# Weight pieces requested from ScalarE's queue, and a new written-out order, in a fused linear-attention and gated-MLP kernel

## The chip, the cores and the metric

The kernel runs on one core of one Trainium2 chip. The metric is the time of one execution on the device, in microseconds (us). The time before is the median of three runs.

## The reference

Two blocks run one after the other, all inputs and outputs in float32.

```python
# block 1: gated linear attention; q, k, v, alpha are (B=4, H=8, S=768, D=48)
for t in range(S):
    state = alpha[:, :, t, :, None] * state + einsum('bhd,bhe->bhde', k[:, :, t], v[:, :, t])
    y[:, :, t] = einsum('bhd,bhde->bhe', q[:, :, t], state)
x = y.transpose(0, 2, 1, 3).reshape(B, S, H * D)          # (4, 768, 384)
# block 2: gated MLP with a spatial product
h = maximum(x @ w_in, 0)                                   # w_in (384, 1024)
u, v = h[..., :512], h[..., 512:]
v_n = (v - mean(v)) / sqrt(var(v) + 1e-6)                  # over the last axis
v_s = einsum('ts,bsd->btd', w_spatial, v_n) + b_spatial    # w_spatial (768, 768)
out = (u * v_s) @ w_out                                    # w_out (512, 384)
```

## The kernel before, in words

**Tiling.** The recurrence is cut into 24 chunks of 128 tokens, six for each of the four batches. The first eight chunks are worked as four pairs (function `pair`), whose loads bring two chunks at once; the other 16 are worked singly (function `first`). A chunk's path is: logarithm of alpha (`lnp` of a pair, `ln` of a single chunk, ScalarE), cumulated sums on TensorE (`cump` or `cum`), exponentials on ScalarE (`einvp`, `eexpp`), products with k and q (`ktp`, `qtp`), transposes of both (`tr.k`, `tr.q`) and their copies out of PSUM (`ev.k`, `ev.q`), scores (`sc`), a mask product on VectorE (`m`, L594 and L765), the output from the scores and v (`ya`), and the share of the state (`y`). The state goes from chunk to chunk by `updq` or `upd` (TensorE), `z` (VectorE, L337 and L339), `S` (a product on GpSimd, L344) and `sb` (its copy to bfloat16). `vbp` casts v. `xs`, `xt` and `xe` turn a chunk's output into the transposed input of block 2.

**Block 2.** Per batch: six groups `v` (three matmuls of 512 columns, L828), whose results get their statistics (`bn`) and are normalised (`rs`, `vn`); eight groups `u` (three matmuls of 384 columns); eight groups `s`, the spatial product (six matmuls of 384 columns, in two parts); a product `g` with u; six groups `o`, the output (four matmuls), and the stores. All these matmuls have line L828.

**Weights.** They come in six pieces of 768 KB: the two halves of `w_in` (`w_in.1`, read by `v`, then `w_in.0`, read by `u`), three thirds of `w_spatial` (`w_sp.0` to `w_sp.2`), and `w_out`. Each is requested by one DMA in `fetch` (L1081), lands in one of two buffers `raw_w`, and is cast to bfloat16 part by part (`cast.w_in.1.0` and so on). There are two buffers, so the third piece is requested when the casts of the first are done, and so on. Each third of `w_spatial` is then transposed on TensorE (`wt.0` to `wt.5`, L840) and copied out (`we`).

**The order.** Nothing is reordered at run time: each engine runs its instructions in the order in which the kernel emits them. That order is written out in the table `PLAN`, made offline; a function `replay` emits operation after operation. A word such as `A4` means operation 4 on ScalarE (P TensorE, D VectorE, A ScalarE, G GpSimd, S the sync engine SP with its queue of requests; Q words emit nothing). The table chooses the engine too where an operation may run on more than one. A suffix gives "junk" columns: `P53:512:512:192` puts three matmuls of those widths on a constant tile, in float32, in front of operation 53, into the PSUM bank that this operation is about to use (L187). They compute nothing that is used. The eight banks are handed out in turn, so an operation waits until the bank's user eight turns earlier is done.

Operations named in the prediction, with their numbers: `cump.0.1` 53, `bb.0` and `bb.1` (the bias row spread over the partitions) 247 and 249, `tr.q.0.0` 51, `S.0` 66, `cz.2` (constants of the single chunks) 3, `sb.0` 67, `sc.1.0` 131, `v.0.0` 85, `u.0.3.0` 155, `v.0.5` 215, `wt.2` 235, `w_in.1` to `w_out` requests 4, 9, 14, 18, 22, 26.

Of the kernel before, what the change touches and what calls it, by code (L numbers as in the profile page):

```python
# [54 lines left out]
LETTERS = {"P": "PE", "D": "DVE", "A": "ACT", "G": "POOL", "S": "SP", "Q": "DMA"}  # L55

PLAN = """
S34 Q35 S36 Q37 G32 G0 Q33 S38 Q39 S94 Q95 S40 Q41 A42 P53:512:512:192 A54 D1 D2 D56 P43 S96 Q97 S98 Q99 S100 Q101
S163 Q164 S4 Q5 S165 Q166 S167 Q168 P59:464 G58 G48 A44 A45 A55 D46 D57 D47 P249:304 P49 P61 A50 P51 D52 D60 A62 A102
A250 P71:304 P74 P113 P103 D72 D73 D76 D75 P63 P77:172 D65 A114 D116 P119:148 A104 A64 A115 A105 A78 G66 G67 G106 D107  # L60
D117 D68 P79 P81 P111 P121 P247 P109 G3 G69 A108 A82 A80 D120 D122 D112 D110 P83 A84 A171 D248 S169 Q170 S9 Q10 S307
Q308 P131 P134 D133 D136 D132 D135 G70 G118 P172:228 P182 P123:240 A183 A8 A173 A124 P137 P138 A139 A174 G7 G6 D125
P85 G126 D128 D185 G127 G129 G175 P88 P142 P140 A86 A184 D176 D186 A143 A89 P188 P190 P180 P144 P178 A141 A191 A145
A181 P146 G11 G12 S309 Q310 S311 Q312 D130 D87 D179 D90 D189 P157 A187 A177 A158 A147 A13 P197 P200 P192 D199 D201
D198 D194 D202 P151:196 P155 A315 A193 A91 P326 P316 A327 P203 P153 P204 G195 G196 G329 A317 A328 A318 P149 A205 A154
D159 D156 D152 D330 G319 P208 P334 A209 P206 D320 P332 P324 P210 P322 D92 D335 D325 D333 D148 A207 P212 A211 A150 P347
P215 P221 A213 A160 A222 A216 S14 Q15 P223 P227 S18 Q19 D93 D323 D161 D348 D349 D214 G16 G17 A224 A228 P225 P229 A226
A21 P232 A234 D231 D230 D233 G20 P235:300 P238 S313 Q314 G331 G321 P344 P336 S367 Q368 S369 Q370 S22 Q23 S371 Q372
A237 A236 D217 D162 D346 A240 D338 A239 A218 D219 D220 A375 A337 P251 P263 P259 P376 A377 A378 G339 P264 D345 D341
D265 P260 D261 P255 P252 A380 A25 A24 D381 D253 P256 D257 G340 G342 G379 S409 Q410 S373 Q374 S446 Q447 S411 Q412 S413  # L70
Q414 S415 Q416 S26 Q27 S480 Q481 S448 Q449 S482 Q483 S450 Q451 S484 Q485 P383 A385 A417 S452 Q453 S577 Q578 S486 Q487
S581 Q582 S579 Q580 S583 Q584 P244 P241 P350 A246 D384 D245 D242 D243 P390 P354 P418 D392 D391 A351 A355 G262 G343
A420 A382 G254 G266 P279 P352 P271 P356 P393 P272 A353 A357 A419 G421 A422 A394 P280 P361 P386 P275 P395 A362 A424
A396 A31 D273 D423 D281 D387 P425 D397 D427 D426 D363 G282 G388 P276 P358 D277 P398 G258 G389 G278 G30 A399 A454 A359
A28 A488 P405 P432 P267 P455 P401 A402 A457 A456 D29 P291 P489 P268 A490 A459 D406 D433 D400 D434 D360 P283 P428 D269
D460 A492 D429 D493 G458 G491 P435 A284 A292 A436 G274 G461 G270 G430 G431 S648 Q649 S617 Q618 S650 Q651 S611 Q612
S652 Q653 S613 Q614 S690 Q691 S615 Q616 S694 Q695 S654 Q655 S692 Q693 P287 P462 P437 P495 P403 D463 D464 D497 D496
A288 A439 A438 P440 A585 A441 A364 D404 P469 P498 P295 P465 P586 P303 D471 D470 D466 D500 D499 A296 A587 A588 A590
A304 P299 G494 G467 G468 G589 G592 D591 D442 P472 A473 P501 P407 P474 A502 A300 P503 P593 P596 A443 A505 A408 D475
D476 P477 A478 D504 D366 D594 D595 D445 D444 D597 D365 P506 P600 P515 D601 D516 A507 A479 A508 D509 D602 A656 A510  # L80
A619 P517 P525 P513 P519 P529 P657 P533 P620 D511 D512 P526 P530 A514 A659 A658 A621 A661 A622 A698 A624 D518 D520
D527 D531 D662 P545 P534 P699 A701 A700 A703 D625 G598 G599 G660 G626 G623 G528 D535 P546 D547 P630 P627 P664 P537
P603 D631 D665 D704 G548 A629 A628 G632 G663 A604 P538 P634 P605 S728 Q729 S762 Q763 S696 Q697 S730 Q731 S732 Q733
S764 Q765 S766 Q767 D539 A607 A666 A606 D635 D636 P541 P667 P542 G702 G532 P706 P671 D668 D543 D673 D672 G669 G536
G670 G544 G633 P608 P637 P521 A707 A736 A708 A638 P737 P713 P639 P522 P549 D714 D715 D641 D523 A770 A609 A705 A738
A739 G740 A640 A741 D742 P771 P550 P642 A772 P709 P744 A774 A643 A746 D710 D551 D775 D745 D644 G524 S858 Q859 S734
Q735 S929 Q930 S860 Q861 G773 G711 G552 G712 G743 G540 P716 P674 A717 A675 P561 P718 P676 P777 P553 A562 A678 A677
D719 D779 D720 D610 P679 P751 A778 A554 A866 A680 A645 A681 P780 D752 P747 D748 D753 D781 D782 P682 P867 P721 P754
A868 A869 A871 A722 A755 S768 Q769 S862 Q863 A723 A776 D683 D872 P573 P688 P684 G749 G750 G870 P756 P874 D646 D757
D875 D685 D758 A689 A574 D724 A876 P686 P783 P569 P881 A784 P785 A570 A787 A687 A725 D882 D786 D883 P759 P557 A760  # L90
P788 P565 P796 P798 P800 S1042 Q1043 S971 Q972 S892 Q893 S864 Q865 S898 Q899 S896 Q897 A979 A558 A789 A566 A937 A900
S894 Q895 S935 Q936 G873 S975 Q976 S931 Q932 S933 Q934 S973 Q974 S977 Q978 S1008 Q1009 S567 Q568 S1046 Q1047 S559 Q560
S1012 Q1013 S1010 Q1011 S1044 Q1045 S1014 Q1015 D727 D647 D761 D726 P794 P806 D790 A791 D799 D797 D795 D792 D793 D801
P901 P980 P802 P938 P877 P807 A902 A903 A907 A905 A981 A939 A940 A982 A944 A984 P810 P803 A942 G904 D878 G941 G879
D808 D906 D804 G805 G880 G809 G983 D985 D943 P822 P884 P811 D812 A885 P823 P908 P886 P945 D824 P814 P911 P815 D912
D909 D816 G813 G817 G913 G825 A910 A887 A888 A947 A946 P889 A1016 A890 P952 P915 P987 D953 D916 D954 P830 P1017 P831
P818 A988 A1019 A1050 A1018 D917 P948 P819 P1051 D949 A1021 A986 A989 D1022 D832 G950 P834 A1052 G951 G1020 P990 P842
P918 A835 A1054 D820 D991 D1055 A843 A919 P838 P1024 P994 P920 D1025 D921 D995 D996 A839 A1023 G914 G833 G1053 G992
S1048 Q1049 S575 Q576 S836 Q837 S844 Q845 S293 Q294 S289 Q290 S571 Q572 S305 Q306 S301 Q302 S555 Q556 A922 A1026 S297
Q298 S285 Q286 S840 Q841 P826 P955 P827 D828 A956 P1057 P957 P1031 D958 P1027 D1028 D1033 D1032 P997 P923 A1058 A1059  # L100
A959 P969 P1060 A1056 A998 P999 D1062 D1001 D1061 D970 G821 G829 G993 G1029 A1000 A924 P960 P846 P1034 A961 A847 G1030
P1063 A1035 A1064 P1002 P963 P1036 P1065 D925 D891 A1003 D962 D1066 P850 P967 A1067 A1037 D1004 A926 D928 P1068 A964
A1038 P1039 D927 D968 A851 A1005 A1069 A1040 D1006 D1041 D1007 D1070 P965 P854 P1076 P1080 P1078 P1074 D966 A1079 A855
A1071 A1081 D1075 D1072 D1073 D1077 P1094 P1082 P1106 P1086 P1083 P1098 P1095 P1090 P1102 P1087 P1107 P1091 P1103
P1110 P1099 P1111 D1096 D1084 G1085 D1088 D1097 D1108 D1092 D1093 G1089 P1113 D1104 G1109 G1105 D1112 D1100 D1101
P1117 P1121 S852 Q853 S563 Q564 S856 Q857 S848 Q849 A1114 S1115 Q1116 A1118 P1133 S1119 Q1120 A1122 P1125 A1134 S1123
Q1124 P1129 S1135 Q1136 A1126 P1137 S1127 Q1128 A1130 A1138 S1131 Q1132 S1139 Q1140
"""


# [13 lines left out]
def kernel(  # L124
# [12 lines left out]
    nc = tc.nc  # L137
# [19 lines left out]
    LD, LP, WT, ST = 1.03, 1.46, 2.35, 0.8  # L157
# [913 lines left out]
    fetched, casts = [], []  # L1071

    def fetch(key, prio, to, src):

        n, cols = src.shape[1], src.shape[2]
        hold = {}

        def load(_):
            flat = raws.tile([128, n * cols], FP32, name="raw_w")
            hold["w"] = flat.rearrange("p (n f) -> p n f", n=n)  # L1080
            nc.sync.dma_start(out=hold["w"], in_=src)  # L1081

        dma(key, WT, load, list(fetched[-NRAW] if len(fetched) >= NRAW else []), prio, issue=0.68)
        for j in range(n):
            tt = 2 * key[-1] + j if to is None else None

            def cast(eng, j=j, tt=tt):
                if to is None:
                    wsp_nat[tt] = raws.tile([128, S], BF16, name="w_row", bufs=NROW)
                copy(eng, wsp_nat[tt] if to is None else to[:, j, :], hold["w"][:, j, :])  # L1090

            op(("cast",) + key + (j,), {"POOL": 0.02 + 0.0012 * cols, "ACT": 0.11 + 0.00073 * cols, "DVE": 0.07 + 0.00104 * cols},
               None, cast, got(key), prio=prio + 12)
            if to is None:
                casts.append((made[("cast",) + key + (j,)], tt))
        made[key] = [made[("cast",) + key + (j,)] for j in range(n)]
        fetched.append(made[key])
# [59 lines left out]
```

## Time and profile before

| | |
|---|---|
| three runs | 143.14, 143.57, 144.17 us; median 143.57 |
| the profiled execution | 143.08 us, of which 141.3 us are the span from the first to the last instruction |
| granted TensorE clock | 1.000 of full |
| TensorE matmul busy | 133.2 us (94% of the span), of it 10.2 us on junk columns |
| VectorE, ScalarE, GpSimd busy | 118.3, 108.6, 83.4 us |
| bytes moved by DMA | 28.64 MB, mean 203 GB/s |

How to read it: busy times are sums of the stretches in which an engine had at least one instruction under way; the junk columns count as busy. Line numbers are those of the kernel file. Durations in the rows reach from an instruction's start to the end of its writes, so that two instructions of one engine can overlap a little.

### The profile page before, as it was taken

The numbers are of one execution on the slowest core, as the hardware profiler recorded it, in microseconds if no ns is written. First come the engines' busy times: TensorE is split into PE (matmuls) and PEld (weight loads), VectorE is DVE, ScalarE is ACT, GpSimd is POOL, SyncE is SP. The second block draws the span as 40 slices with busy tenths as digits, with TensorE's granted clock in tenths as the row PEclk, the third lists the DMA queues.
The fourth block names the chain that finished last, engine by engine and source line by source line (L and its number), as shares of the span: only waits on it lengthen the run. The fifth ranks groups of instructions, "written<-read, shape, count | busy, mean of one in ns | idle before, by whom it ended". The sixth has DMA issues, their size and how long they took to land.

```text
span 141.3 us, 4968 instructions
## 1 busy us (share of the span) xinstructions
PE 133.2 (94%) x1912; PEld 84.2 (60%) x1923; DVE 118.3 (84%) x291; ACT 108.6 (77%) x282; POOL 83.4 (59%) x146
## 2 busy tenths in 40 slices
PE   7989798999999999999999999999999989999990
PEld 3457575575667656565675665656666656566560
DVE  7479878999989599999998898989979779894940
ACT  3677569988989969889887999997889969940061
POOL 6722986293449596982299899500799993000720
PEclk9999999999999999999999999999999999999999
DMA  4999999999898989989799999979978690112044
GB/s 102 323 323 332 331 272 311 225 320 238 241 232 156 283 161 208 205 161 212 154 205 179 193 217 177 222 143 195 250 151 203 225 375 24 70 56 102 0 164 170
DMA packets 89000, 28.64 MB, mean 203 GB/s; under 512 B 83728, under 2 KB 87440, under 8 KB 88976
## 3 DMA queue, kind: packets, MB, share of 16 engines
q1 hardware_dynamic: 88944, 28.32, 81.6%
q8 instruction: 15, 0.25, 0.7%
q14 instruction: 9, 0.07, 0.2%
q0 software_dynamic: 32, 0.00, 0.0%
HBM read 23.60 MB, written 4.72 MB: 200 GB/s over the span
## 4 chain that ended last, share of the span: by engine, by line
PE 71%; DVE 9%; POOL 7%; issue 5%; ACT 4%; ACTq 0%; POOLq 0%; DVEq 0%
PE bank L828 47%; PE bank L187 4%; DVE ptm L594 3%; PE bank L719 2%; PE bank L754 2%; POOL sbd L199 2%; POOL gT L989 2%; PE bank L511 2%; PE bank L782 2%; DVE ptm L765 2%; PE bank L740 1%; PE bank L583 1%; POOL kt L690 1%; PE bank L666 1%; DVE kqT L199 1%
## 5 line engine op out<-in xcount | busy, mean ns | idle before, releaser
L828 PE MATMUL bank<-w_spT,vn 128*128 128x384 bf16 x192 | 36.8, 326 | 0.0
L989 POOL TENSOR_TENSOR gT<-vsb,uT 128x384 bf16<-128x384 f32 x28 | 25.7, 923 | 14.9 <-DVE vsb L976 14.4
L690 POOL TENSOR_TENSOR kt<-kc,binv 128x384 bf16<-128x384 f32 x16 | 14.6, 914 | 13.4 <-ACT bc L685 8.6
L765 DVE TENSOR_TENSOR ptm<-bank,mask 128x512 bf16<-128x512 f32 x32 | 20.7, 682 | 1.9 <-PE bank L398 1.2
L828 PEld LDWEIGHTS <-vn 128*128 128x128 bf16 x192 | 16.6, 97 | 9.5 <-issue 0.2
L976 DVE TENSOR_TENSOR vsb<-bank,bsp_bc 128x384 f32<-128x384 f32 x31 | 16.5, 551 | 4.2 <-PE bank L828 2.5
L828 PE MATMUL bank<-xT,w_in 128*128 128x384 bf16 x96 | 18.7, 326 | 0.0
L828 PE MATMUL bank<-w_out_sb,gT 128*128 128x384 bf16 (+1 forms) x100 | 18.7, 319 | 0.0
L828 PE MATMUL bank<-w_in,xT 128*128 128x512 bf16 x61 | 17.2, 379 | 0.8 <-issue 0.2
L344 POOL TENSOR_TENSOR state<-state,bc 128x192 f32<-128x192 f32 x20 | 10.4, 520 | 11.4 <-DVE state L337 5.4
L197 ACT COPY kqT<-bank 128x512 bf16<-128x512 bf16 x21 | 12.1, 599 | 3.9 <-PE bank L719 1.1
L199 POOL CAST sbd<-state 64x192 bf16<-64x192 f32 x38 | 13.3, 350 | 2.0
L893 DVE BATCH_NORM_STATS2 stats<-v_sb 128x6 f32<-128x512 bf16 x20 | 13.7, 683 | 0.3 <-ACT v_sb L203 0.3
L203 ACT ACTIVATE v_sb<-bank 128x512 bf16<-128x512 f32 x20 | 11.8, 605 | 1.4 <-PE bank L828 1.3
L197 ACT CAST x_sb<-bank 128x384 bf16<-128x384 f32 x24 | 11.4, 490 | 1.5 <-PE bank L623 1.3
L828 PEld LDWEIGHTS <-w_in 128*128 128x128 bf16 x96 | 8.8, 97 | 5.9
L828 PEld LDWEIGHTS <-gT 128*128 128x128 bf16 x100 | 8.9, 97 | 5.6 <-DVE gT L989 0.4
L199 DVE COPY kqT<-bank 128x512 bf16<-128x512 bf16 x27 | 10.5, 416 | 1.9 <-PE bank L511 1.0
L187 PE MATMUL bank<-junk 128*128 128x512 f32 (+9 forms) x24 | 10.2, 529 | 1.1 <-DVE junk L240 1.1
L594 DVE TENSOR_TENSOR ptm<-bank,mask 128x512 bf16<-128x512 f32 x16 | 10.2, 683 | 0.5 <-PE bank L583 0.4
L197 ACT COPY xT<-bank 128x192 bf16<-128x192 bf16 (+1 forms) x26 | 9.4, 379 | 1.6 <-PE bank L398 1.1
L197 ACT COPY o_sb<-bank 128x384 f32<-128x384 f32 x9 | 4.4, 484 | 8.0 <-PE bank L828 8.0
(126 smaller groups left out, 284.0 us busy)
## 6 DMA issues: line engine op xcount, KB each, us to landing
ac<-in_alpha_dram SPq DMA_DIRECT2D x16, 192.0 KB, 4.1
kc<-in_k_dram SPq DMA_DIRECT2D x16, 192.0 KB, 4.8
qc<-in_q_dram SPq DMA_DIRECT2D x16, 192.0 KB, 4.1
vc<-in_v_dram SPq DMA_DIRECT2D x16, 192.0 KB, 3.8
raw_w<-in_moe_w_spatial_dram SPq DMA_DIRECT2D x3, 768.0 KB, 6.8
out_dram<-raw_w SPq DMA_DIRECT2D x11, 192.0 KB, 2.5
out_dram<-o_sb SPq DMA_DIRECT2D x9, 192.0 KB, 1.8
ac<-in_alpha_dram SPq DMA_DIRECT2D x4, 384.0 KB, 5.0
```

Source lines behind the costliest of these rows:

```text
L187: nc.tensor.matmul(out=flat[:, 0:cols].rearrange("p (a b) -> p a b", a=4), lhsT=junk, rhs=junk[:, None, 0:n].to_broadcast([128, 4, n]), st ...
L197: nc.scalar.copy(out=out, in_=in_)
L199: ENG[eng].tensor_copy(out=out, in_=in_)
L203: nc.scalar.activation(out=out, in_=in_, func=AF.Relu)
L344: ENG[eng].tensor_tensor(out=st["state"], in0=st["state"], in1=st["bc"][:, :, None].to_broadcast([128, HP, D]), op=ALU.mult)
L594: nc.vector.tensor_tensor(out=st[f"ptm{par}"][:, s], in0=st[f"pt{s}{par}"], in1=mask2[:, par], op=ALU.mult)
L690: ENG[eng].tensor_mul(out=k_blocks(kt3)[:, :, :, 0:D], in0=quad(st["kc"]), in1=st["binv"])
L765: nc.vector.tensor_tensor(out=st["ptm"][:, s], in0=st[f"pt{s}"], in1=mask4, op=ALU.mult)
L828: return lambda ps: nc.tensor.matmul(out=out(ps), lhsT=lhsT(), rhs=rhs(), start=start, stop=stop)
L893: nc.vector.bn_stats(out=stats, in_=d["v_sb"][:, tt, :])
L976: nc.vector.tensor_tensor(out=hold["vs"], in0=ps[:, 0:TH], in1=bsp_bc[:, th, :], op=ALU.add)
L989: ENG[eng].tensor_tensor(out=bt[b]["gT"][:, dsl, cols], in0=hold["vs"], in1=bt[b]["uT"][:, dsl, cols], op=ALU.mult)
```

## The change

Two edits. First, the six requests for weight pieces are issued by ScalarE, on ScalarE's own queue of requests, and no longer by SP; the table's maker is told 0.43 us for such a request instead of 0.68. Second, `PLAN` is a new table over the same 1141 operations. By its description the maker of the table now counts the time in which VectorE is held by GpSimd, and places junk columns by the gaps of the new order. Of the operations that may run on several engines, 12 copies `ev` move from VectorE to ScalarE and 8 the other way, 8 `u` to ScalarE and 2 back, 8 small `xe` to ScalarE and 7 back, 4 copies `sb` and 3 products `g` from GpSimd to VectorE and one of each back, and 4 weight casts from ScalarE to GpSimd. The junk suffixes after the first are 464, 304, 304, 172, 148, 228, 240, 196 and 300 columns before, the last at `wt.2`; after, they are 512:512:512 at `tr.q.0.0`, then 320, 292, 224 and 204, the last at `sc.1.0`.

```diff
@@ PLAN, its first lines
-S34 Q35 S36 Q37 G32 G0 Q33 S38 Q39 S94 Q95 S40 Q41 A42 P53:512:512:192 A54 D1 D2 D56 P43 S96 Q97 S98 Q99 S100 Q101
-S163 Q164 S4 Q5 S165 Q166 S167 Q168 P59:464 G58 G48 A44 A45 A55 D46 D57 D47 P249:304 P49 P61 A50 P51 D52 D60 A62 A102
-A250 P71:304 P74 P113 P103 D72 D73 D76 D75 P63 P77:172 D65 A114 D116 P119:148 A104 A64 A115 A105 A78 G66 G67 G106 D107
-D117 D68 P79 P81 P111 P121 P247 P109 G3 G69 A108 A82 A80 D120 D122 D112 D110 P83 A84 A171 D248 S169 Q170 S9 Q10 S307
...
+G32 G0 S34 Q35 D2 Q33 S38 Q39 D1 S36 Q37 S94 Q95 S40 Q41 A42 P247:512:512:192 P249 A250 P53 S96 Q97 P43 A54 A55 A248
+S98 Q99 A44 A45 D46 S163 Q164 A102 D47 D57 P51:512:512:512 D56 S100 Q101 P61 A48 G58 A52 P63:320 S167 Q168 P59 D65 P49
+D62 A60 S165 Q166 A50 P74:292 A64 P103 A4 Q5 D76 G66 P71 S169 Q170 A171 G3 D72 A104 D68 S307 Q308 D73 A105 G106 P113
+P172 D75 A114 P182 G67 D107 A183 G69 D116 A173 P111:224 P109 A115 P77 A184 G108 D117 P81 G7 D112 A78 A174 G6 S311 Q312
+D186 P79 P119 A80 D176 G118 P190 A82 D120 G8 P121 S309 Q310 D110 P180 A122 G175 D181 A191 D185 P131:204 G70 P83 P85
...
@@ fetch, load
-            nc.sync.dma_start(out=hold["w"], in_=src)
-
-        dma(key, WT, load, list(fetched[-NRAW] if len(fetched) >= NRAW else []), prio, issue=0.68)
+            nc.scalar.dma_start(out=hold["w"], in_=src)
+
+        dma(key, WT, load, list(fetched[-NRAW] if len(fetched) >= NRAW else []), prio, "ACT", 0.43)
```

## The prediction

> **What bounds the kernel now.** I read the page's first two parts, then the chain that ended last, then stretches of the span, then the waits.
>
> ```profile
> span 141.3 us, 4968 instructions
> PE 133.2 (94%) x1912; PEld 84.2 (60%) x1923; DVE 118.3 (84%) x291; ACT 108.6 (77%) x282; POOL 83.4 (59%) x146
> PEclk9999999999999999999999999999999999999999
> ```
>
> TensorE is busy 94% of the span, at full granted clock. Its end decides: in the chain, in order of time, the last long piece is TensorE alone, and after it come one copy and the last store.
>
> ```profile
> 120.12 17.56 PE bank L828 x105
> 137.72 0.31 issue
> ```
>
> Stretches of five and twenty us, with their sum, then TensorE, weight loads, VectorE, ScalarE and GpSimd; the first group is everything, the second only the junk matmuls of L187:
>
> ```profile
> 25.00:30.00 5.00, 4.66 (x103) 3.17 (x103) 4.93 (x12) 4.42 (x12) 1.92 (x5) 1.00 0.96 270
> 35.00:40.00 5.00, 4.86 (x119) 3.18 (x118) 4.51 (x13) 4.97 (x14) 1.73 (x3) 1.00 0.94 245
> 40.00:60.00 20.00, 19.90 (x309) 12.55 (x309) 17.95 (x44) 16.91 (x44) 16.21 (x26) 1.00 0.97 204
> 80.00:100.00 20.00, 19.61 (x267) 12.35 (x267) 18.10 (x48) 18.70 (x56) 10.46 (x18) 1.00 0.99 195
> ...
> 5.00:10.00 5.00, 2.62 (x8) 0.95 (x6) 1.00 1.17 324
> 35.00:40.00 5.00, 0.77 (x2) 0.30 (x2) 1.00 0.94 245
> ```
>
> Busy time of pipelined matmuls does not show whether they are packed, so I made a **ledger**: each TensorE operation at the price it has when its neighbours follow at once. 380 matmuls of 384 columns at 0.163 us (the timeline has twelve in 2.11, less the 0.16 by which the last outlives its slot) are 62.0; 72 of 512 columns at 0.215, 15.5; the attention chunks, from the chain's pieces (16 single chunks at 1.5 to 1.7, four pairs at 4.1), 43.5; weight transposes, bias rows and the last halves 2.5. Sum 123.5. In the old table 22.7 of it stands ahead of `wt.2`, which starts at 37.43 after the last junk; 100.7 are left, and TensorE ends at 137.7, 100.3 later. So **from 37 us on nothing is to be gained but small change, and much can be lost; the first 37 us hold 14.7 us without useful matmuls**, 5 of them before the first input can be used.
>
> The weight requests are hardly waited for: in all waits, these are the two lines.
>
> ```profile
> POOL w_in L199 <- DMA raw_w<-in_moe_w_in_dram: 1.1, 1, 1.1
> ACT w_out_sb L197 <- DMA raw_w<-in_moe_w_out_dram: 0.8, 1, 0.8
> ```
>
> **The requests.** SP loses six instructions that took 0.37 to 1.6 us each. Its queue has slack: the loads that it brings wait for free buffers later on, and only two waits on loads, 2.2 and 2.8 us, both before 9.3 us, are in the trace. I give the freed SP time nothing. No trace of before shows a request on ScalarE. From below: 0.37, the shortest `w_spatial` request on SP, six times, 2.2 us in all. From above: an SP request behind others, which lasts until the queue takes it.
>
> ```profile
> 10.17 1.33 SPq L1081 DMA_DIRECT2D raw_w<-in_moe_w_in_dram  x1
> 11.55 0.49 SPq L441 DMA_DIRECT2D kc<-in_k_dram  x1
> 12.08 1.07 SPq L441 DMA_DIRECT2D qc<-in_q_dram  x1
> 13.19 3.79 SPq L441 DMA_DIRECT2D vc<-in_v_dram  x1
> ```
>
> An empty queue is nearer to SP's first request, 0.42, or the 0.49 above, than to 3.79; I take 0.45, in all 2.7 us. They stand between ScalarE's operations, which have 0 to 0.6 us of slack per 5 us from 20 to 40: what waits behind each is a PSUM copy that TensorE needs. The casts moved from ScalarE to GpSimd (0.65, 0.65, 0.84 and 0.51 by their rows, 2.65 together) pay for it on the whole, so its sum stays near 109.
>
> **A wait that is new on ScalarE** is the one for a `raw_w` buffer, which SP bore. Only `w_sp.1` comes early enough to bite: it needs the casts of `w_in.0`, now on VectorE and GpSimd, and behind it stand `v.0.3`'s copy and `xe.4`.
>
> **When a piece lands.** On SP it took 5.5 to 7.1 us from the request, most of it behind earlier loads. In a queue of its own it meets the same 16 DMA engines, which are at work all the time until 110 us. 768 KB at the 330 GB/s of the first 20 us take 2.4 us alone, 4.8 at half: 3 to 7.1, and I take 4.8.
> [...]
>
> **The order table, first 37 us.** I followed the new words by hand with the old rows: on ScalarE each operation of 384 columns follows the last after 0.38 and is ready after 0.49; `lnp` 0.73 and 0.85; copies `ev` 0.48 and 0.60; on VectorE masks 0.60 and 0.68, `ktp` and `qtp` 0.48 and 0.55, `ev` 0.34 and 0.41; on GpSimd `ktp` 0.91, `S` 0.5, `sb` 0.72, casts of `w_in` 0.6. First `bb.0` and `bb.1` now stand ahead of `cump.0.1`: 5.14 becomes 5.37. On ScalarE `be.1` and `be.0` stand among the exponentials, so `qtp.0.0` is ready at 8.6 and not 8.0; the 1536 junk columns (2.56 us at the rate of later junk) cover that wait. The scores come after `updq.0`, so the first mask starts at 12.2 against 10.1, while `S.0` starts at 12.3 against 13.0. `cz.2` (1.41) and `ktp.1.0` stand ahead of `sb.0`: the first use of the state comes at 16.5 against 14.5. `sc.1.0` comes at 19.2 against 16.5. In return pair 2 is prepared early: `v.0.0` starts at 19.7 (old 20.2, and `w_in.1` must land by 17), `ya.2` at 26.9 against 29.2. Then VectorE is full (masks, statistics, two casts of `w_in.0`) and `u.0.3.0` stands still for 1.0 us until 29.2; `v.0.5` ends at 33.9 with 19.9 of the ledger done. The old one ends it at 34.0 with 20.3.
>
> **The sum.** Behind `v.0.5` 103.6 are left: 137.5. `wt.2` is due at 35.2; `w_sp.1` is requested at 29.6 behind the last cast of `w_in.0`, lands at 34.4 by 4.8 us, and its two casts of 0.83 on GpSimd make `wt.2` and `wt.3` wait 0.5 together (nothing at 3 us, 2.5 at 7.1). TensorE ends at 138.0, 0.3 later than 137.7. The new tail has the same four groups `o` and the same halves behind the last `s`, so I keep the 3.6 us after TensorE. Against the profiled execution 143.08 + 0.3 = 143.4; that one lies 0.49 below the median of the runs, so **143.9**. A hand-over by hand may miss 0.03 us forty times, 1.2 us; its own range is 142.3 to 145.2.
>
> **VectorE held by GpSimd.** One row shows it: the product of two float32 tiles, minimum, median and maximum in ns.
>
> ```profile
> L989 DVE TENSOR_TENSOR gT<-vsb,uT x3: 549/559/1093, 131.2 to 135.2; 128x384 bf16<-128x384 f32 x3
> ```
>
> It nearly doubles once. The masks, from PSUM, stay at 680 to 692. So few instructions here can be held, and counting it makes a plan little truer; two more such products on VectorE in the tail cost 0.56 to 1.09 each, under 1.95 us of `o` groups.
>
> **Rivals.**
> 1. *Packed from the start, faster.* The new table has no junk behind `sc.1.0`, as if its maker saw no gaps there. From 19.2 the ledger has 116.3 left: 135.5, 2.2 less; 141.4. For it: the old table is packed where it has no junk. Against: 30 to 35 has none either, and my walk finds VectorE full at 29. 0.29.
> 2. *A request on ScalarE is held while SP's is under way, slower.* SP's requests last 3.79, 4.11, 3.52 and 4.40 us between 13 and 34; if one must end before ScalarE's can begin, the four pieces before 30 us wait 0.6, 1.5, 1.5 and 1.5 (about half of those durations, rounded down), 5.1, of which ScalarE's slack takes 1 to 2: 147. It decides from 0.5 us a request. For it: SP's requests run nearly back to back. Against: no second queue is in the trace. 0.14.
> [...]
> 3. *Weights late in GpSimd's order, slower.* Behind `cast.w_in.1.1` stand `ktp.2.0` and `sb.1`, behind the casts of `w_sp.0` stands `ktp.3.1`. At 7.1 us a piece, `v.0.0` comes 1 us later, `ktp.3.1` 1 and `wt.2` and `wt.3` 2.5, of which about 2.5 add up: 146.1. Against: 7.1 held behind a full queue. 0.17.
> 4. *The pieces are hidden anyway* is in the forecast, 0.40.
>
> **Chances.** Faster by over 1%, about what a measurement of this kernel tells from no change: 0.29 and a little of the forecast, 0.30. Slower: rivals 2 and 3, 0.31. Within: 0.39. The range, 140.7 to 147.2, leaves out about a tenth at each end.
>
> **What would show it.** Right: six requests on ScalarE under 0.6 us, landing in 3 to 5.5; `sc.1.0` near 19, `v.0.5` ending near 34, packed TensorE after. Wrong: a ScalarE request of several us (rival 2), GpSimd waiting over 1 us for `raw_w` (3), no gap near 29 (1), or new TensorE gaps after 40 us, for which I have no step.

## The result and the profile after

The changed kernel takes 148.38 us (median; 147.98 to 149.00) against 143.39 for the kernel before on the same chip: a ratio of 1.034, 95% interval 1.0285 to 1.0398. The prediction, 143.9 with a range of 140.7 to 147.2 and "within 1%" as the likeliest case, was wrong. From here on, medians and ratios leave out executions more than 1.5% slower than the fastest of their kernel (two each of e3 and e9, one each of e2 and e5), and a ratio can differ a little from the quotient of the medians.

The profiled execution took 148.57 us, its span is 5.5 us longer than before's. The page's first parts, then the end of the chain:

```profile
span 146.8 us, 4951 instructions
PE 135.9 (93%) x1904; PEld 84.1 (57%) x1919; DVE 122.4 (83%) x294; ACT 109.1 (74%) x281; POOL 83.2 (57%) x144
PEclk9999999959999999999999999999999999999998
```

```profile
126.27 16.90 PE bank L828 x102
143.22 0.31 issue
```

TensorE still sets the end, but ends at 143.2 instead of 137.7, and its clock dips once, near 30 us. Stretches of the same kind as before (TensorE, weight loads, VectorE, ScalarE, GpSimd; clock, DMA share, GB/s); the last line is the junk alone:

```profile
25.00:30.00 5.00, 3.52 (x108) 2.91 (x108) 4.33 (x10) 3.40 (x8) 3.63 (x8) 1.00 1.11 349
30.00:35.00 5.00, 4.78 (x61) 2.86 (x63) 4.42 (x9) 3.75 (x12) 3.09 (x4) 0.66 0.77 158
40.00:60.00 20.00, 19.68 (x330) 12.64 (x331) 18.95 (x47) 16.31 (x43) 12.42 (x21) 1.00 1.00 228
80.00:100.00 20.00, 19.48 (x326) 12.59 (x328) 18.27 (x44) 17.61 (x47) 15.16 (x27) 1.00 0.97 195
...
5.00:10.00 5.00, 3.21 (x8) 1.11 (x6) 1.00 1.17 325
```

Behind 40 us TensorE is nearly as dense as before. The hole is at 25 to 30 (3.52 of 5 us, before 4.66), followed by a clock of 0.66. From the list of all waits, three of TensorE's (who waits, for whom; us in total, times, longest) and the one on the weights:

```profile
PE bank L374 <- issue: 1.5, 1, 1.5
PE bank L461 <- DVE state L339: 1.0, 1, 1.0
PE bank L828 <- POOL w_in L199: 0.8, 1, 0.8
...
POOL w_in L199 <- DMA raw_w<-in_moe_w_in_dram: 2.0, 2, 1.3
```

None of the three TensorE waits is in before. The longest has no releaser ("issue": the profile shows nothing that it waited for): TensorE stood still inside a group of three transposes whose inputs were there. The requests themselves, on ScalarE's queue (minimum, median, maximum in ns), were as cheap as forecast, and landed late:

```profile
L1081 ACTq DMA_DIRECT2D raw_w<-in_moe_w_spatial_dram x3: 374/375/384, 25.2 to 39.5; - x3
L1081 ACTq DMA_DIRECT2D raw_w<-in_moe_w_in_dram x2: 374/398/422, 12.4 to 21.2; - x2
...
DMA to landing us min/median/max: 5.0/5.9/7.2
```

Two places of the timeline (start, length, engine, line, operation) hold most of what follows: the stall, and two VectorE operations beside two of GpSimd.

```profile
27.18 0.22 PE L374 MATMUL bank<-ident,x_sb 128*128 128x128 bf16 x1
28.88 0.44 PE L374 MATMUL bank<-ident,x_sb 128*128 128x128 bf16 x5 [1.48 <-issue]
...
32.01 1.69 POOL L199 CAST w_row<-raw_w 128x768 bf16<-128x768 f32 x2
32.26 1.56 DVE L199 CAST sbd<-state 64x192 bf16<-64x192 f32 x2
33.67 0.92 POOL L483 TENSOR_TENSOR kt<-kc,binvp 128x384 bf16<-128x384 f32 x1
33.85 1.22 DVE L925 TENSOR_SCALAR vn<-v_sb,mvs,rstd 128x512 bf16<-128x512 bf16 x2
```

**Two landmarks** order all that follows: the starts of `sc.0.1` (the first scores) and of `v.0.5` (the last `v` group of batch 0). They cut each span into a head (up to `sc.0.1`), a stretch (from there to `v.0.5`) and the rest.

### The profile page after: what moved, and what is told of

The parts are those of the page before. It is cut to its first block, busy times and chain, and to the rows that moved or that the text cites. A ratio compares the mean times of both kernels' runs of the same rounds, so it can differ in the third digit from the quotient of the medians.

```text
span 146.8 us, 4951 instructions
## 1 busy us (share of the span) xinstructions
PE 135.9 (93%) x1904; PEld 84.1 (57%) x1919; DVE 122.4 (83%) x294; ACT 109.1 (74%) x281; POOL 83.2 (57%) x144
## 4 chain that ended last, share of the span: by engine, by line
PE 63%; DVE 16%; DMA 7%; ACT 5%; issue 4%; POOL 3%; ACTq 0%; POOLq 0%
PE bank L828 40%; DMA raw_w<-in_moe_w_in_dram 5%; PE bank L187 3%; PE bank L754 3%; PE bank L719 2%; DVE vn L925 2%; DMA ac<-in_alpha_dram 2%; DVE stats L893 2%; PE bank L740 2%; PE bank L782 2%; DVE ptm L594 2%; DVE sbd L199 2%; PE bank L666 2%; PE bank L398 2%; PE bank L776 1%
## 5 line engine op out<-in xcount | busy, mean ns | idle before, releaser
L828 PE MATMUL bank<-w_spT,vn 128*128 128x384 bf16 x192 | 36.0, 326 | 0.0
L989 POOL TENSOR_TENSOR gT<-vsb,uT 128x384 bf16<-128x384 f32 x26 | 23.5, 915 | 16.0 <-DVE vsb L976 15.6
L828 PEld LDWEIGHTS <-vn 128*128 128x128 bf16 x192 | 17.2, 97 | 10.7 <-issue 0.2
L828 PE MATMUL bank<-w_in,xT 128*128 128x512 bf16 x57 | 17.7, 398 | 2.0 <-POOL w_in L199 0.8
L828 PE MATMUL bank<-xT,w_in 128*128 128x384 bf16 x96 | 19.2, 326 | 0.0
L197 ACT COPY kqT<-bank 128x512 bf16<-128x512 bf16 x25 | 13.8, 591 | 5.2 <-PE bank L719 3.1
L199 POOL CAST sbd<-state 64x192 bf16<-64x192 f32 x32 | 11.6, 362 | 1.7
L203 ACT ACTIVATE uT<-bank 128x384 bf16<-128x384 f32 x20 | 9.4, 492 | 3.8 <-PE bank L828 3.2
L925 DVE TENSOR_SCALAR vn<-v_sb,mvs,rstd 128x512 bf16<-128x512 bf16 x24 | 9.7, 440 | 1.7 <-ACT rstd L918 1.6
L187 PE MATMUL bank<-junk 128*128 128x512 f32 (+5 forms) x20 | 9.8, 617 | 1.1 <-DVE junk L240 1.1
```

What stands on the lines that cost most here:

```text
L187: nc.tensor.matmul(out=flat[:, 0:cols].rearrange("p (a b) -> p a b", a=4), lhsT=junk, rhs=junk[:, None, 0:n].to_broadcast([128, 4, n]), st ...
L197: nc.scalar.copy(out=out, in_=in_)
L199: ENG[eng].tensor_copy(out=out, in_=in_)
L203: nc.scalar.activation(out=out, in_=in_, func=AF.Relu)
L828: return lambda ps: nc.tensor.matmul(out=out(ps), lhsT=lhsT(), rhs=rhs(), start=start, stop=stop)
L925: nc.vector.tensor_scalar(out=d["vn"][:, t, :], in0=d["v_sb"][:, t, :], scalar1=d["mvs"][:, t, 0:1], scalar2=d["rstd"][:, t:t + 1], op0=AL ...
```

## The experiments

**Which half of the change.** The old order with the requests on ScalarE where the old words had them for SP, and the new order with the requests still on SP:

```diff
-            nc.sync.dma_start(out=hold["w"], in_=src)
+            nc.scalar.dma_start(out=hold["w"], in_=src)   # e1: with the old PLAN, S4 -> A4 and so on
-A4 Q5 ... A9 Q10 ...
+S4 Q5 ... S9 Q10 ...                                  # e2: the new PLAN, nc.sync as before
```

> The old order with the six weight requests moved to ScalarE's queue, at the same places in the overall order. Theory R (the requests cost the time: pieces on a second queue take the DMA engines from the loads and from TensorE's own instruction blocks): 145.5 to 148, with a TensorE gap of over 1 us or a half-clock stretch somewhere before 45 us. Theory O (the new order costs it): 143 to 144.5, within 1% of before. If ScalarE's six requests are as cheap as in the changed kernel (0.37 to 0.42 us each), their own cost is under 1 us.

Measured: 151.78 us, ratio 1.061 (1.0557 to 1.0663).

> The new order with the six requests back on SP's queue, at the same places in the overall order. Theory R: 143 to 145, no gap of 1.5 us at the transposes of x_sb near 28 us and no half clock after it. Theory O: 147 to 149, as the changed kernel. If both share it: about 146.

Measured: 148.46 us, ratio 1.0358 (1.0332 to 1.0385): the order alone costs as much as the whole change. Alone, the requests cost more still, for a reason of place. SP issues loads long before they are used, while ScalarE comes to the same word of the table only when its work is done: `w_sp.0` was requested at 35.5 us instead of 24.1, and TensorE stood still for its transposes (a line of the timeline, and one of the waits).

```profile
35.52 0.38 ACTq L1081 DMA_DIRECT2D raw_w<-in_moe_w_spatial_dram  x1
```

```profile
PE bank L840 <- POOL w_row L199: 5.1, 2, 4.8
```

The request took 0.38 us; the kernel is 8.5 us slower. So I tried the old order with each request at a place in ScalarE's order that comes near the time at which SP had issued it (two words for casts, G16 and G17, also stand earlier in the table; GpSimd's own order is the same):

```diff
-... S4 Q5 ... S14 Q15 S18 Q19 ... S22 Q23 ...
+... A102 A4 Q5 ... A191 A14 Q15 ... A315 A18 Q19 ... A213 A22 Q23 ...
```

> The old order with the six requests on ScalarE, but placed in ScalarE's order where SP had issued them by the clock (w_in.1 near 10.2 us, w_in.0 17, w_sp.0 24, w_sp.1 28, w_sp.2 34, w_out 43) instead of at the places of SP's words, where w_sp.0 came at 35.5 and the kernel took 151.8. If a request on ScalarE costs only its 0.4 us and the place decides: 143 to 144.3, no change. If a second queue costs by itself (its packets take bandwidth from the loads, instruction blocks come late), 145 or more, with new TensorE waits on loads before 37 us or a stall without a releaser.

Measured: 145.21 us (144.24 to 146.25), ratio 1.0109 (1.0054 to 1.0164). Place was most of it, but not all: about 1% is left, and the time lies in the second of the two ranges expected. In the profiled execution the clock dips, and VectorE waits for a load, which it did not before:

```profile
PEclk9999959999999999999999999999999999999999
```

```profile
DVE qt L490 <- DMA qc<-in_q_dram: 1.3, 1, 1.3
```

The three other runs had the full clock and lay at 144.24 to 145.31, so the dip is not the whole of that 1%; how the rest divides I did not separate.

**The old table up to `wt.3`, then the new one.**

```diff
+PLAN = old words up to P238 (wt.3), then the new table's words that are left, requests on SP
```

> The old order up to the transposes wt.3, then all operations that are left in the new order, requests on SP. If the new order loses only in the first 37 us: 142.5 to 144.5. If its later part loses too, as the 0.8 us between the ledger and the end of the changed kernel suggests: 144 to 145.5.

Measured: 145.19 us, ratio 1.0151 (1.0111 to 1.0192). TensorE was short at the seam (4.43 us of 35 to 40, 18.92 of 40 to 60) and packed after it (20.00 of 60 to 80). That is 1.9 us over before, in the second range expected, against 5.2 for the whole new order: with the old head 3.3 of them are gone, so most of the new order's loss belongs to its first 37 us. How much of the 1.9 the seam itself makes stays open.

**What the stall is.** Theory F: TensorE ran out of instructions. They come by DMA in blocks, and the page's list of queues has a row for them (packets, MB, share of the DMA engines' time):

```profile
q8 instruction: 15, 0.25, 0.7%
```

The page counts 3823 TensorE instructions (1904 matmuls, 1919 weight loads); if the fifteen blocks of 16 KB are theirs, a block holds some 255. In the trace the second block of the span started only at 26.61 us (before: 19.41) and took 0.93; TensorE stopped at 27.4, some 700 instructions into its stream (349 matmuls and 352 weight loads up to 27.5, behind the first of `xt.2`'s transposes), and went on at 28.9. With the order alone, the same stream, it stopped behind the same transpose (block at 26.09). Rivals, as what sets the time: W, `w_in.1` lands late for GpSimd; V, VectorE is full and held by GpSimd (its instruction lasts until one of GpSimd beside it has ended: above, `sb.4`'s two casts to 33.82, GpSimd's two to 33.70). Two edits that only shift the stream, then one for W, one for F by earlier packets, one for V:

```diff
-P247:512:512:192 ... P53                        # e3
+P247:512:192 ... P53, with 32 small matmuls of 64 columns ahead of it
-P51:512:512:512                                 # e8
+P51, with 44 small matmuls of 64 columns ahead of it
-... A44 A45 D46 ... P103 A4 Q5 ...              # e5
+... A44 A45 A4 Q5 D46 ... P103 ...
-... A4 Q5 D76 ... A84 A9 Q10 ...                # e6
+... A4 Q5 A9 Q10 D76 ... A84 ...
-D11 ... D12 D196 ... D24                        # e7
+G11 ... G12 G196 ... A24
```

> The changed kernel with 64 more TensorE instructions at its start: 32 small bfloat16 matmuls with their weight loads ahead of the first cumulated sum, in place of one junk matmul of 512 columns. Theory F (TensorE ran out of fetched instructions at 27.4 us): the gap of about 1.5 us comes some 64 instructions earlier in the program, so it no longer splits the transposes of x_sb of chunk 2 or 3; 147 to 149.5. Rival (the gap belongs to that operation: a wait that the profile does not show): it stays between the same transposes, at the same length.

Measured: 147.11 and 148.78 us, ratio 1.0324 (1.025 to 1.0398). The stall at `xt.2` was gone, but the full clock came only at 10.8 us in the profiled execution, which hid what that was worth; it is not in the table below.

> The changed kernel, with one word of the table moved: the request of w_in.1 stands behind the first pair's second exponential on ScalarE and is issued near 9 us instead of 12.4. Theory W (w_in.1 comes late for GpSimd's casts, and all that follows is late by it): GpSimd no longer waits 1.3 us for the piece, v.0.0 runs through from about 20.5, v.0.5 ends 1 to 1.5 us earlier, 147.2 instead of 148.4. Theory F (the stall without a releaser at xt.2 and the half clock behind it set the end): v.0.0 comes earlier, and the time falls by less than 0.5, since the stall at xt.2 stays. If the piece's packets push aside loads that the head needs, sc.0.1 or cump.1.1 comes later and the gain is lost there.

Measured: 148.26 us, ratio 1.0353 (1.0301 to 1.0406). The wait at `v.0.0` went and most of the stall (0.3 left), but `sc.1.0` came later (21.1 instead of 20.5) and TensorE waited 1.2 us each for a copy by VectorE and one by GpSimd: no gain. W alone is not the bound.

> The changed kernel, with the request of w_in.0 moved right behind that of w_in.1, to near 12.8 us instead of 21.2. Theory F: the packets of w_in.0 no longer run between 23 and 28 us, so the 16 KB block of instructions that started at 26.6 comes earlier, TensorE does not stand still inside xt.2 and the clock stays full from 30 to 33.4: 2 to 3 us less, 145.5 to 146.5. Theory V (VectorE full and held by GpSimd's casts from 30 to 37 us): the stall may go, but the casts and masks of that stretch stay, so v.0.5 ends less than 1 us earlier: 147.5 or more. Theory W: two pieces at once land later, w_in.1 by 1 to 2 us, and the time grows by as much.

Measured: 148.36 us, ratio 1.0347 (1.0282 to 1.0412). Neither stall nor half clock, and yet no gain: F alone is not it, and V came nearest, which had said 147.5 or more.

> The changed kernel, with four operations given back the engines that they had in the old table: the copy sb.4 and the two casts of w_in.0 that VectorE had go to GpSimd, one cast of w_sp.2 goes from VectorE to ScalarE. VectorE loses about 3 us of work between 30 and 38 us. Theory V: u.0.3.0 and wt.1 come about 1 us earlier and the time falls by 0.7 to 1.5, to 147 or 147.7. Theory F: no change over 0.3. If GpSimd's casts become the late ones, u.0.x waits for GpSimd instead, and the time grows by up to 1.

Measured: 147.86 us (147.31 to 149.23), ratio 1.0317 (1.0256 to 1.0377): 0.5 less, which this scatter does not tell from nothing, with the stall of 1.4 us and a new wait for GpSimd's `w_row` of 1.1. Here V gets no support from the time.

> The changed kernel, with the 1536 junk columns ahead of tr.q.0.0 cut into small bf16 matmuls of 64 columns, 44 instead of three, which take about the same time but put some 80 instructions more ahead of all that follows on TensorE. Theory F: the stall belongs to a place in the stream of instructions (the end of a fetched block), so it leaves xt.2 and comes some 80 instructions earlier, or goes where TensorE waits anyway; the half clock at 30 to 33 us goes with it, and the time falls by 2 or so. Theories W and V: the stall, if any, stays at xt.2, or its going changes the time by less than 0.5, since VectorE and the late casts set the end of v.0.5.

Measured: 145.63 us, ratio 1.0158 (1.012 to 1.0196): 2.8 us less, for matmuls that compute nothing (2.3 of it in the stretch of the profiled execution). The block came at 20.3 and the six transposes ran through. What else went is in the timeline (in this kernel line numbers are four higher):

```profile
25.89 0.58 PE L378 MATMUL bank<-ident,x_sb 128*128 128x128 bf16 x6
...
30.34 0.52 DVE L203 CAST sbd<-state 64x192 bf16<-64x192 f32 x2
30.90 0.74 DVE L929 TENSOR_SCALAR vn<-v_sb,mvs,rstd 128x512 bf16<-128x512 bf16 x2
31.97 1.59 POOL L203 CAST w_row<-raw_w 128x768 bf16<-128x768 f32 x2 [1.94 <-DMA raw_w<-in_moe_w_spatial_dram]
```

VectorE got to its two casts before GpSimd had the piece to cast: 0.52 instead of 1.56, and 0.74 instead of 1.22 for the two `vn`. In the kernel with the second piece early, whose stall was gone too, GpSimd was 0.05 us ahead of it:

```profile
31.44 1.62 POOL L199 CAST w_row<-raw_w 128x768 bf16<-128x768 f32 x2 [0.36 <-DMA raw_w<-in_moe_w_spatial_dram]
31.49 1.68 DVE L199 CAST sbd<-state 64x192 bf16<-64x192 f32 x2
```

**So is the hold what ate the gain?** Four kernels on that: the second piece early with `w_sp.0` cast on ScalarE; small matmuls and second piece early; both with that cast; and then, to see whether stall and VectorE add up, the relief of VectorE with each way of being rid of the stall.

```diff
-... G16 ... G17 ...       # e9 (on e6), e11 (on e10); e10 is e6 and e8 together
+... A16 ... A17 ...
-... D76 ... D72 ... D68 ...  # e15, on e13 (e8 and e7); e14 is e6 and e7
+... D76 ... D68 D72 ...
```

> The kernel with w_in.0 requested early (which had neither the stall at xt.2 nor the half clock, and still took 148.36), with the two casts of w_sp.0 moved from GpSimd to ScalarE. Theory V, in a sharper form: a float32-to-bf16 cast or a bf16 normalisation on VectorE that runs beside a cast or float32 product on GpSimd lasts until that one ends. Then the two casts of sb.4 on VectorE take 0.5 instead of 1.68, the two vn 0.75 instead of 1.2, the wait for sbd (0.8) and the one for kqT inside wt.1 (0.7) go, and the time falls by 1 to 1.6, to 147. The rival: those operations are long because VectorE's inputs come late, or the end is set by GpSimd's other work; then sb.4 stays over 1.2 us and the time within 0.4 of 148.4. ScalarE gets 1.65 us more work between 31 and 34; if that is what sets the end, the time grows by up to 1.

Measured: 147.63 and 147.72 us, ratio 1.0304 (1.0248 to 1.036), inside the scatter of e6 (147.49 to 149.05). A miss in time and a hit in mechanism: `sb.4` took 0.52 and the two `vn` 0.73, but the hold only moved, to a cast of `w_in.0` (1.16; 0.42 in the changed kernel) beside GpSimd's `ktp.3.1`, which now stood earlier, and ScalarE, stuck in order behind its new casts, made TensorE wait 1.5 us for `xT`.

```profile
30.33 0.91 POOL L483 TENSOR_TENSOR kt<-kc,binvp 128x384 bf16<-128x384 f32 x1
30.36 1.16 DVE L199 CAST w_in<-raw_w 128x512 bf16<-128x512 f32 x1
31.55 0.52 DVE L199 CAST sbd<-state 64x192 bf16<-64x192 f32 x2
```

> Both edits that took the stall at xt.2 away, together: 44 small matmuls in place of the junk ahead of tr.q.0.0 (145.63 alone), and w_in.0 requested right behind w_in.1 (148.36 alone). If the gains add, GpSimd's wait of 1.9 us for w_in.0 and TensorE's 1.1 for sbd in the former go: 144.6. If VectorE's hold by GpSimd decides (theory V), the casts of w_sp.0 come early too and fall on sb.4 again, which was 0.52 us in the former and 1.68 in the latter: 146 to 146.8, worse than the 145.63.

Measured: 146.33 us, ratio 1.0209 (1.0163 to 1.0256): V's figure, worse than the small matmuls alone. Up to `u.0.3.0` it is 0.2 us ahead of them; from there to `v.0.5` it takes 6.34 us instead of 4.83, with `sb.4` at 1.56 and the `vn` at 1.22 again.

> The same, and the two casts of w_sp.0 on ScalarE. By theories F and V together no stall and no hold are left before v.0.5: v.0.5 starts near 34 instead of 38.1 in the changed kernel, and as everything behind it has cost 108.6 to 108.7 of span in all kernels of the new order, the span is 142.7 and the time 144.3 to 144.6, within 1% of before's. If a loss of the new order is left that neither theory names, the time stays at 145.6 or above.

Measured: 148.01 us, ratio 1.032 (1.0278 to 1.0362): a miss by over 3 us. `sb.4` is free, but the same cast of `w_in.0` is held (1.17, and TensorE waits 1.0 for it), TensorE waits 1.5 us for ScalarE's `xT` as above, and the head is 1.1 longer than in e10.

> The changed kernel with w_in.0 requested right behind w_in.1 (148.36 alone: no stall, but sb.4 held for 1.68 us and a wait of 0.7 for kqT) and the same four operations off VectorE. Theory V: VectorE's hold was all that ate the gain of the missing stall; without it 1.0 to 1.9 less, 146.5 to 147.4. The rival, that the early piece delays the loads and the end depends on them: 148 or more.

Measured: 147.71 us (146.23 to 147.81), ratio 1.0286 (1.023 to 1.0341). The median is 0.65 lower, less than V's 1.0 to 1.9; but the profiled execution has a head 1.2 us longer, and its stretch is 1.67 shorter, as V had it.

> The changed kernel with two edits that were tried alone: the 44 small matmuls in place of the junk ahead of tr.q.0.0 (145.63: no stall at xt.2), and the copy sb.4, two casts of w_in.0 and one of w_sp.2 off VectorE (147.86, with the stall still there). If VectorE bounds the stretch before v.0.5 once the stall is gone: 0.5 to 1.2 less than 145.63, 144.4 to 145.1. If GpSimd, which takes three of the four and was waited for by 1.08 us there, is the bound: 145.6 to 146.6.

Measured: 146.70 us, ratio 1.0236 (1.0203 to 1.0269). No gain where the hold was already gone, and just above the second range expected: the stretch is the same within 0.1, GpSimd's casts are waited for 1.2 us, and the head is 0.9 longer.

> The first of these kernels, with one word moved: z.1 stands ahead of the mask m.0.0.0 on VectorE instead of behind it. TensorE waits 1.04 us for z.1 ahead of cump.1.1 in every kernel of the new order; z.1 can start when GpSimd has S.0, 0.7 earlier. If that wait is on the path: 0.4 to 0.7 less than the first kernel. If the 224 junk columns and the waits behind it cover it: the same within 0.3.

Measured: 145.96 us, ratio 1.0187 (1.0154 to 1.0219). The wait for `z.1` fell from 1.04 to 0.33, but 0.7 came back in front of junk columns; the stretch is 0.27 shorter, so that wait is mostly covered. The median is 0.74 under e13's, which alone would put the wait on the path; but in the profiled executions 0.34 of the 0.83 between the two spans is the head, which lies ahead of that wait.

The landmarks of the profiled executions, in us (rest: from the start of `v.0.5` to the end of the span; in the kernels with the relief, `sb.4` is on GpSimd):

| kernel | `sc.0.1` | `v.0.5` | stretch | rest | stall at `xt.2` | `sb.4` and the two `vn` on VectorE |
|---|---|---|---|---|---|---|
| before | 9.81 | 33.36 | (other order) | 107.9 | no | other order |
| changed | 12.80 | 38.09 | 25.29 | 108.7 | 1.48 | 2.78 |
| e2, order only | 11.98 | 37.89 | 25.91 | 108.5 | 1.02 | 2.79 |
| e5, first piece early | 12.73 | 37.76 | 25.03 | 108.6 | 0.29 | 2.90 |
| e6, second piece early | 13.06 | 37.44 | 24.38 | 108.6 | no | 2.89 |
| e7, relief | 12.70 | 37.64 | 24.94 | 109.8 | 1.45 | `vn` 1.16 |
| e8, small matmuls | 12.19 | 35.14 | 22.95 | 108.7 | no | 1.26 |
| e9, e6 and casts on ScalarE | 12.51 | 37.26 | 24.75 | 108.6 | no | 1.25 |
| e10, e6 and e8 | 12.06 | 36.41 | 24.35 | 108.6 | no | 2.78 |
| e11, e10 and casts on ScalarE | 13.12 | 37.69 | 24.57 | 108.6 | no | 1.25 |
| e13, e8 and relief | 13.12 | 36.00 | 22.88 | 109.0 | no | `vn` 1.19 |
| e14, e6 and relief | 14.23 | 36.94 | 22.71 | 109.1 | no | `vn` 1.18 |
| e15, e13 and `z.1` | 12.78 | 35.39 | 22.61 | 108.8 | no | `vn` 1.18 |

With the stall gone, `sb.4` not held (or moved) and ScalarE's order left alone, the stretch is 22.6 to 23.0, reached by two roads (e8, and e6 with the relief); with one of the two left it is 24.3 to 24.9; with both, 25.0 to 25.9. That is what shows that **both** cost, and why taking one away can bring nothing: the stall makes VectorE late, and a VectorE that is no longer late meets GpSimd's cast. The kernels e9 and e11 are the exception: free of the stall and of the hold on `sb.4`, they stay at 24.6 to 24.8. Their casts on ScalarE bring waits of their own, and another cast is held; that these make up the whole difference was not tested. Nothing tried is faster than the kernel before.

## Where the 5.5 us of span went

- **Head, 0.6 to 0.8.** `sc.0.1` starts at 12.0 to 12.2 in the new-order kernels whose full clock came by 4.8 us, and at 12.80 here, where it came at 6.09 (before: 4.81). In the profiled executions the start of the full clock lies anywhere from 4.35 to 10.77 with the new order and from 4.24 to 7.28 with the old, so I do not count it as the change's; with one profile for each kernel that is not proven.
- **Stretch, 2.3 to 2.7.** 25.29 against the 22.6 to 23.0 of the kernels without the stall and the hold on `sb.4`.
- **The order itself up to `v.0.5`, some 1.3.** Head 12.0 and stretch 22.7 make 34.7; before's `v.0.5` starts at 33.36. (The kernels at 22.7 have further edits, so this is an estimate.)
- **Behind `v.0.5`, 0.8.** 108.7 against 107.9. From 60 to 80 us TensorE is busy 19.34 instead of 19.83; I did not trace it further.

## Why the prediction was wrong, step by step

The step that failed is the walk of the new words between 19 and 34 us. It had `u.0.3.0` starting at 29.2 and `v.0.5` ending at 33.9; measured, `u.0.3.0` starts at 33.52 and `v.0.5` at 38.09. It had no term for a TensorE that stands still with its inputs there (1.48 us here), and it put the hold of VectorE by GpSimd at nothing. The details, in the order of the prediction:

**Requests, 0.45 us each: right** (0.37 to 0.42), and the rival of a request held behind SP's is out: none took longer, not even the one at 25.2, inside an SP request that lasted 4.08 from 23.00. (One of the durations that rival was priced from, 3.52, is two weight requests in one row.) The new wait for a `raw_w` buffer on ScalarE did not show: its semaphore rows ahead of the requests last 38 ns at most.

**When a piece lands, 4.8 us: too short** (5.0 to 7.2). No run shows the 3 us at the low end of its range, which the sum puts beside a `wt.2` that waits for nothing: the shortest landing of a piece is 5.0 here and 4.4 with the order alone, on SP's queue. `w_in.1`, due "by 17" in the walk, came at 19.6, and `v.0.0` waited 0.8. The third rival had named this and put 2.5 us on it; but the early piece (e5) shows that to take the wait away gains nothing. The sum's 0.5 for `wt.2` and `wt.3` did not come: `w_sp.1` was requested at 32.7 and landed at 38.0, but TensorE has no wait for its casts.

**The walk of the new words.** With a head on time (the order alone) it held to 0.5 us up to 19 us: `y.1` 16.95 for 16.5, `sc.1.0` 19.67 for 19.2. It failed in the next 12 us: `ya.2` came at 31.31 for 26.9 (30.35 in the order alone, 27.84 with the small matmuls). The forecast had "1.0 idle" there for a full VectorE, and no step by which TensorE stands still with its inputs there. That stall was 1.48 of the 4.4; 0.8 was the late head and 0.8 the wait for `w_in`; the rest is in small waits and, from 29.98 on, the half clock. Without stall and hold `v.0.5` would still start some 1.3 later than before (the estimate above), where the walk had it end 0.1 earlier: some of the order's own cost was missed too, and which hand-overs make it up stays open.

**"VectorE held by GpSimd ... few instructions here can be held": the other failed step.** I looked for it in one form, the product of two float32 tiles. The new table puts three more copies `sb` (six casts) on VectorE, and they are the worst case. One form in the changed kernel, then in before (minimum, median, maximum in ns):

```profile
L199 DVE CAST sbd<-state x8: 255/772/876, 32.3 to 118.2; 64x192 bf16<-64x192 f32 x8
```

```profile
L199 DVE CAST sbd<-state x2: 255/326/398, 22.8 to 23.2; 64x192 bf16<-64x192 f32 x2
```

Free 0.26, held 0.77. Two other forms are held in the rows above: the two `vn` take 1.22 us here beside GpSimd's product `kt` and 0.74 in e8, ahead of GpSimd's casts, and in e9 a cast of `w_in.0` takes 1.16 beside that product (0.42 in the changed kernel). The forecast should have priced every form that a row shows long beside GpSimd; why VectorE is held no row shows. So a table that counts this hold can still run into it: where the weights land by the clock, and not as planned, decides what stands beside what.

**Behind `v.0.5`: nearly right.** 0.4 more was forecast (138.0 less 33.9 against 137.7 less 34.0), 0.8 came. The ledger's view, that all depends on the first 37 us, held; the 1.2 us that the range allowed for missed hand-overs were far too few for it. The first rival's sign, no gap near 29, failed at once.

## What to carry to other kernels

A walk by hand with busy times holds while each engine waits only for what the table names; add a line for what it doesn't name (here a stall that fits a late block of instructions, 1.48 us; a VectorE cast beside GpSimd, 0.77 us instead of 0.26; a piece's landing, 5.0 to 7.2 us), and price it by the stretch with least slack. Before an order is blamed or praised, shift its code by a few dozen instructions that do nothing (here the time fell by 2.8 us in e8, but not clearly in e3): if 2 us come or go, the order alone is not what was measured. A request that moves from a queue that runs ahead to an engine that works in order must be placed by the clock (151.78 us at SP's places in e1, 145.21 by the clock in e12).

## What the runs showed of the hardware

- TensorE probably ran out of instructions: it stood still for 1.48 us with no wait that the trace shows. The last 256 matmuls and weight loads before the stop (127 and 129) passed in some 4.4 us (23.05 to 27.4), while the next block started at 26.61, when weight packets were under way, and took 0.93; TensorE went on 1.3 us after it had ended. In all four kernels with this stall it went on 1.3 to 1.5 us after the block's end (1.33 here, 1.51 with the order alone, 1.33 in e5, 1.27 in e7); in e6 the block ended at 26.47, and TensorE passed the place 1.54 later without a stop. That the block is what it waited for is inferred from these times and from the three edits that moved them (e3, e6, e8); what passes between the block's end and the next matmul no row shows.
- The clock went to half for one or two periods of 3.41 us, at whole multiples of 3.41 from the first full clock: after 23.89 us here (7 periods), 13.65 in e12 (4), 34.13 in e1 (10, and for two periods). The period before the dip had TensorE idle throughout in e1, but busy 57% of the time here and 72% in e12, while 57% in e7 kept the full clock: busy time in these periods alone doesn't decide, and what does was not shown. The dip seems to have cost little: with the order alone, which has a stall of 1.02 us and no dip, the stretch is 0.6 us longer than here.
